# A new planned order of loads, squares and stores in a DMA-heavy attention and mixture-of-adapters kernel: 16 stores in place of 19

## The chip, the cores and the metric

The kernel runs on one core of a Trainium2 chip. The metric is the device time of one launch in microseconds (us); lower is better. The core's engines are called PE (TensorE, matmul), PEld (its weight loads), DVE (VectorE), ACT (ScalarE), POOL (GpSimd) and SP (SyncE); 16 DMA engines move data between device memory (HBM) and the on-chip memory.

## The reference

```python
B, N, C = (4, 6400, 256)                     # q, k, v: float32 [B, N, C]
def _attn_ref(q, k, v, tau):
    qn = q / (np.linalg.norm(q, axis=1, keepdims=True) + 1e-06)
    kn = k / (np.linalg.norm(k, axis=1, keepdims=True) + 1e-06)
    s = kn.transpose(0, 2, 1) @ qn / tau     # [B, C, C]: attention between channels
    s = s - s.max(-1, keepdims=True)
    a = np.exp(s)
    a /= a.sum(-1, keepdims=True) + 1e-09
    return (v @ a).astype(np.float32)

def _moe_ref(x, w_gate, A, B):               # x = attention output as [25600, 256]; 8 experts, rank 16
    logits = x @ w_gate
    topk = np.argpartition(-logits, K, axis=1)[:, :K]          # K = 2
    ...
    w = np.exp(sel)                          # sel: the two chosen logits less their maximum
    w /= w.sum(-1, keepdims=True) + 1e-09
    ...
            z = x[mask] @ A[e]
            delta[mask] += w[mask, k, None] * (z @ B[e])
    return (x + delta).astype(np.float32)
```

Per batch, a 256x256 matrix of products of k and q is summed over all 6400 rows, divided by the column norms of k and q, and turned into a softmax `a`. Then each row of v is multiplied by `a`, and a gated sum of two of eight rank-16 adapters is added.

## The kernel before

**Layout.** The 6400 rows of a batch lie on 128 partitions, 50 rows ("columns" below, 256 numbers each) per partition. q and k of a batch come in two halves of 25 columns (`QK`); v and the output are cut into 5 pieces of 10 columns (`PC` = 10, `NP` = 5). A piece is written (b, i): batch, number in the batch. One column is 128 KB in float32.

**Loads.** Every load of q, k and v but the first two goes out on POOL's queue (L690) and turns float32 into bf16 on the way; the profile counts its bytes on the bf16 side. `WORDS` is the order of the loads: q31 is the second half of q and k of batch 3, v12 the third load of v of batch 1. `V` says which pieces one load of v brings: (2, 2) is pieces 2 and 3 in one load of 20 columns. `PARTS` cuts a half of q and k into several loads. A load waits on POOL until its slot is free: there are 4 slots for halves of q and k, and 4 for pieces of v.

**Batch stage.** For each column, PE adds the product of k and q to an accumulator (step `G`, L705). The squares for the norms come in one of two ways, chosen per batch, group of five columns and q or k: as further matmuls of `G` (L709 for k, L713 for q), or, for the entries of `OFF`, as a Square on ACT (L726) and an addition on DVE (L732), summed up at the end and brought in by a small matmul (`n2p`, L747). After the last column a chain of small steps on PE, DVE and ACT makes the softmax `a` and `waA`, that is `a` times gate weights and adapters.

**Piece stage.** Per piece: transposes of v on PE (`T`, L890) and their copy out (L872 on ACT or L874 on DVE); gate logits and adapter inputs in one go, twenty matmuls (`ZL`, L914), for pieces in `MERGED`, otherwise logits first (`log`, L928) and the adapter inputs later (`Z`, L981); the gate on DVE and ACT; the gated inputs (L992); their transposes (`gzT`, L1004); then per two columns the output, v times `a` plus the adapters (`Y`, L1017 and L1022), and its copy into one of 7 output slots (`Ye`, L872 or L874).

**Stores.** A store (L1033) goes out on SP's queue. A piece in `PAIRS` is stored together with the next one, in one store of 20 columns from two neighbouring slots. `FINE` cuts pieces of the last batch into several stores. `HOLD` names a load, and the store is not issued until that load has landed:

```python
def held_by(p, b, i):
    kind, d, j = HOLD[b, i]
    return [k for k in p.steps if k[:4] == ("load", kind, d, load_of(d, j) if kind == "v" else j)][-1]
```

(0, 3): ('k', 3, 1) thus holds piece (0, 3) until the second half of k of batch 3 has landed; with kind 'v' the third number is a piece, and the load is the one that brings it.

**The order.** All of it is laid out when the program is built. `Plan.run` is a list scheduler with given costs: each engine takes, of the steps that are ready and find their slots free, the one with the lowest rank. A rank is a place in the order of loads: `G` has the place of its half, the steps of a piece that of its load, and the early steps of a piece (`T`, `ZL`, the gate) that place less `AHEAD`; squares have the place of their half less `SQ`. The engines then run the order so found, waiting on semaphores. Where PE has nothing to do the plan puts matmuls whose result nobody reads (`warm`, L880).

```python
p.add(("T", b, i, u), {"PE": 0.109 * n + 0.001}, [("load", "v", b, v, c0 * PC, n0 * PC)], x - ahead, ...)
p.add(("sq", w, b, g), {"ACT": 0.106 + 0.2133 * n}, ..., pos["qk", b, i] - SQ, ...)
...
parts = FINE[i] if b == B - 1 and i in FINE else ((0, PC * len(names)),)
for c, n in parts:
    p.add(("store", b, i, c, n), {"SP": 0.46}, ...)
```

Of the kernel before, what the change touches and what calls it, by code (L numbers as in the profile page):

```python
# [71 lines left out]
class Plan:  # L72
# [35 lines left out]
    def run(self, head):  # L108
# [137 lines left out]
UNITS = ((0, 4), (4, 4), (8, 2))  # L246
GATE = {"eq1": "ga", "t": "ga", "th": "ga", "g2": "ga", "lm": "gb", "mask": "gb"}
QK = ((0, 25), (25, 25))
V = (((0, 1), (1, 1), (2, 2), (4, 1)), ((0, 1), (1, 1), (2, 1), (3, 2)), ((0, 1), (1, 1), (2, 1), (3, 1),
        (4, 1)), ((0, 1), (1, 1), (2, 2), (4, 1)))  # L250
PAIRS = {(0, 1), (1, 0), (2, 0), (2, 3)}

GROUPS = ((0, 5), (5, 5), (10, 5), (15, 5), (20, 5), (25, 5), (30, 5), (35, 5), (40, 5), (45, 5))
ZUNITS = ((0, 3), (3, 3), (6, 2), (8, 2))
# [3 lines left out]
def group_of(c):  # L258
    return max(g for g, (c0, _) in enumerate(GROUPS) if c0 <= c)
# [6 lines left out]
def load_of(b, i):  # L266
    return max(g for g, (i0, _) in enumerate(V[b]) if i0 <= i)


def pieces(b, i):  # L270

    return next((((b, j), (b, j + 1)) for j in (i - 1, i) if (b, j) in PAIRS), ((b, i),))
# [8 lines that stand above are left out]
def make_plan(B, order, ahead):  # L281
# [6 lines left out]
    for kind, b, i in order:  # L288
        if kind == "v":
            c0, n = V[b][i]  # L290
            p.add(("load", "v", b, i, c0 * PC, n * PC), {}, (), 0, take=(("v", tuple((b, c0 + j) for j in range(n))),),
                  size=COL * n * PC)
            continue
        for c, n in PARTS.get((b, i), QK[i:i + 1]):
            for h in "qk":
# [3 lines left out]
    for h in "qk":  # L299
        p.add(("cast", h), {"ACT": 1.2}, [("load", h, 0, 0) + PARTS[0, 0][0]], 0)  # L300
    for b in range(B):

        for i, (c0, n) in enumerate(QK):
            for c in range(c0, c0 + n):
                deps = [k for k in p.steps if k[0] == "load" and k[2:4] == (b, i) and k[1] != "v"
                        and k[4] <= c < k[4] + k[5]]
                if (b, c) < (0, PARTS[0, 0][0][1]):
                    deps = [("cast", k[1]) for k in deps]
                if c:
                    deps.append(("G", b, c - 1))  # L310
                elif b:
                    deps += [(x, b - 1, ic) for x in ("n2", "accs") for ic in range(2)]
                p.add(("G", b, c), {"PE": 0.445 - 0.1135 * sum((b, group_of(c), w) in OFF for w in "kq")}, deps,
                      pos["qk", b, i] if b else -50,
# [3 lines left out]
        for w in "kq":  # L318
            halves = [x for x in range(len(GROUPS)) if (b, x, w) in OFF]
            if halves:  # L320
# [3 lines left out]
            for x, g in enumerate(halves):  # L324
# [3 lines left out]
                      [k for k in p.steps if k[:4] == ("load", w, b, i) and k[4] < c + n and c < k[4] + k[5]]  # L328
                      + [("cast", w)] * ((b, c) == (0, 0)), pos["qk", b, i] - SQ, take=(("ssq", ((w, b),)) if x == 0 else ("sq", ((w, b, g),)),),
                      give=(("qk", (w, b, i)),))  # L330
                if x:
                    p.add(("add", w, b, g), {"DVE": 0.069 + 0.2668 * n},
                          [("sq", w, b, g), before], pos["qk", b, i] - SQ, give=(("sq", (w, b, g)),))
                    before = ("add", w, b, g)
# [6 lines left out]
        if b == 0:  # L341
            p.add(("wts",), {"DVE": 2.12}, [("load", "k", 0, len(QK) - 1) + PARTS[0, len(QK) - 1][1]], -200)

# [21 lines left out]
        for i in range(NP):  # L365
            v = load_of(b, i)
            c0, n0 = V[b][v]
            x = pos["v", b, v] + 0.3 * (i - c0)
            for u, (c, n) in enumerate(UNITS):
# [4 lines left out]
                      [("T", b, i, u)], x - ahead, give=(("bank", ("T", b, i, u)),))  # L374
            merged = (b, i) in MERGED
            if merged:
# [54 lines left out]
    for b in range(B):  # L431
        for i in range(NP):
            x = pos["v", b, load_of(b, i)]
            names = pieces(b, i)
            if (b, i) != names[0]:
                continue
            parts = FINE[i] if b == B - 1 and i in FINE else ((0, PC * len(names)),)
            for c, n in parts:
                p.add(("store", b, i, c, n), {"SP": 0.46},
                      [("Ye", b, i + c0 // PC, c0 % PC) for c0 in range(c, c + n, 2)]  # L440
                      + ([held_by(p, b, i)] if (b, i) in HOLD else []), x, size=COL * n,
                      give=tuple(("y", x) for x in names) if c + n == PC * len(names) else ())
# [3 lines left out]
def make_order(words):  # L446

    order = [("qk", 0, i) for i in range(len(QK))]
    for w in words.split():
        order.append(("v" if w[0] == "v" else "qk", int(w[1]), int(w[2])))  # L450
    return order


WORDS = ('q10 v00 q11 v01 v02 q20 v03 v10 q21 v11 v12 v13 q30 v20 v21 v22 v23 q31 v24 v30 v31 v32 v33')
HEAD = 5.05
COL = 1.024 * 1.17647 / 32
WARM = 150
AHEAD = 5.7

HOLD = {(0, 0): ('v', 3, 2), (0, 1): ('v', 1, 4), (0, 2): ('v', 1, 2), (0, 3): ('k', 3, 1), (1, 0): ('v', 2,  # L460
        4), (1, 1): ('k', 3, 2), (1, 2): ('k', 3, 1), (1, 3): ('v', 3, 1), (2, 0): ('v', 3, 3), (2, 1):
        ('k', 2, 0), (2, 2): ('v', 1, 3), (2, 3): ('v', 2, 2), (3, 3): ('v', 2, 2)}

PARTS = {(0, 0): ((0, 5), (5, 12), (17, 8)), (0, 1): ((25, 17), (42, 8)), (3, 1): ((25, 17), (42, 8))}
FINE = {3: ((0, 6), (6, 4)), 4: ((0, 4), (4, 4), (8, 2))}
SPLIT, SHARES = set(), ()
OFF = {(0, 0, 'k'), (0, 0, 'q'), (0, 1, 'k'), (0, 2, 'k'), (0, 2, 'q'), (0, 3, 'k'), (0, 4, 'k'), (0, 4,
        'q'), (0, 5, 'q'), (0, 6, 'k'), (0, 7, 'k'), (0, 9, 'q'), (1, 0, 'k'), (1, 2, 'k'), (1, 3, 'k'), (1,
        3, 'q'), (1, 6, 'k'), (1, 6, 'q'), (1, 7, 'q'), (1, 8, 'k'), (1, 9, 'k'), (2, 0, 'k'), (2, 1, 'k'),
        (2, 3, 'k'), (2, 3, 'q'), (2, 4, 'k'), (2, 5, 'k'), (2, 5, 'q'), (2, 6, 'k'), (2, 6, 'q'), (2, 7,  # L470
        'q'), (2, 8, 'q'), (2, 9, 'q'), (3, 0, 'k'), (3, 1, 'k'), (3, 2, 'k'), (3, 2, 'q'), (3, 3, 'q'), (3,
        5, 'k'), (3, 5, 'q'), (3, 7, 'q'), (3, 8, 'q'), (3, 9, 'q')}
SQ = 0
SAFE = 1.3
MERGED = {(0, 0), (0, 1), (0, 2), (0, 3), (0, 4), (1, 0), (1, 1), (1, 2), (1, 3), (1, 4), (2, 0), (2, 2),
        (2, 3), (2, 4), (3, 0), (3, 1), (3, 2), (3, 3), (3, 4)}


def first_ahead(nc, names):
# [90 lines left out]
def kernel(  # L570
# [72 lines left out]
    scrap = const.tile([1, 16], BF16, name="scrap")  # L643
    order = make_order(WORDS)
    plan = make_plan(B, order, AHEAD)
    steps = plan.run(HEAD)
# [5 lines left out]
    def sb(s, kind, name, shape, dtype, part=""):  # L652

        if (kind, name, part) not in held:
            held[kind, name, part] = sbuf.tile(
                shape, dtype, tag=f"{kind}{at[kind, name]}{part}", name=f"{kind}{part}")
        return held[kind, name, part]
# [41 lines left out]
    def do_G(s, b, c):  # L699
# [4 lines left out]
        for ic in range(CC):  # L704
            nc.tensor.matmul(  # L705
                acc[ic][:, 0:256], kt[:, j, ic::CC], qt[:, j, :],
                start=c == 0, stop=False, skip_group_check=True)
            if (b, group_of(c), "k") not in OFF:
                nc.tensor.matmul(  # L709
                    acc[ic][:, 256:384], kt[:, j, ic::CC], kt[:, j, ic::CC],  # L710
                    start=False, stop=False, skip_group_check=True)
        for ic in range(0 if (b, group_of(c), "q") in OFF else CC):
            nc.tensor.matmul(  # L713
# [42 lines left out]
    def do_n2(s, b, ic):  # L756
# [5 lines left out]
        for x, w in enumerate("kq"):  # L762
            if all((b, g, w) in OFF for g in range(len(GROUPS))):
                continue
# [6 lines left out]
    def do_rsqrt(s, b):  # L771
        n2 = st[b]["n2"]
        for x, w in enumerate("kq"):
            part = held.get(("bank", ("n2p", w, b)))
            if part is None:
                continue
            if all((b, g, w) in OFF for g in range(len(GROUPS))):
                nc.vector.tensor_copy(n2[:, x, :], part)
# [97 lines left out]
    def do_cast(s, what):  # L876
        nc.scalar.copy(held["qk", (what, 0, 0), ""][:, 0:PARTS[0, 0][0][1], :], W[what])  # L877

# [23 lines left out]
    def gate_tiles(s, b, i):  # L902
        for part in ("log", "ga", "gb"):
            sb(s, "gate", (b, i), [P, PC, E], FP32, part)
        for part in ("m1", "m2", "msum"):
            sb(s, "gate", (b, i), [P, PC], FP32, part)
# [30 lines left out]
    def gate_step(name):  # L937
        def f(s, b, i):
            if (b, i) in MERGED and name == "m1":
                gate_tiles(s, b, i)  # L940
            g = {part: held["gate", (b, i), GATE.get(part, part)]
                 for part in ("log", "m1", "eq1", "lm", "m2", "msum", "t", "th", "mask", "g2")}
            if (b, i) in MERGED:
                g["log"] = held["zl", (b, i), ""][:, :, 0:E]
# [41 lines left out]
    def do_Ze(s, b, i, u):  # L986
        c, n = UNITS[u]
        gz = sb(s, "gz", (b, i, u), [P, n, ER], BF16)
        z = held["zl", (b, i), ""][:, c:c + n, E:] if (b, i) in MERGED else held["bank", ("Z", b, i, u)]
        pairs = gz.rearrange("p c d -> p (c d)").rearrange("p (h x two) -> p h two x", two=2, x=ER)  # L990
# [37 lines left out]
    def do_store(s, b, i, c, n):  # L1028
# [3 lines left out]
        for rows in SHARES if (b, i) in SPLIT else (P,):  # L1032
            r = nc.sync.dma_start(out_v[b, p:p + rows, lo:lo + n, :], Y[p:p + rows, at_y:at_y + n, :])  # L1033
            if (b, i) in HOLD and not p:
                tc.add_manual_dep(r.ins, loaded[held_by(plan, b, i)],
# [62 lines left out]
```

## Time and profile before

| | |
|---|---|
| time of the kernel, median of 3 runs | 251.12 us (251.01 to 251.16) |
| span of the profiled execution, first to last instruction | 246.2 us |
| around the span, to the median | 4.9 us (the last store is issued at 244.8 us and lands in 5.1 us) |
| busy PE, DVE, ACT | 218.3, 184.8, 169.7 us |
| DMA | 65.85 MB in 8788 packets as the queues count it; HBM read 78.91 MB, written 26.21 MB |
| loads on POOL's queue | 39: 17 of v, 11 of q, 11 of k |
| stores on SP's queue | 19: 4 of 20 columns, 10 of 10, 1 of 6, 3 of 4, 1 of 2 |
| mean granted TensorE clock | 0.965 |

The profile is of one execution. Its view by slices cuts the span into 40 parts and gives the busy share of each engine in tenths, then that of the DMA engines and what they moved; one DMA engine can hold packets of two queues at a time, so that a share can be over 1. The view by windows gives busy microseconds per engine in stretches of our choice, the granted clock, the DMA share and GB/s. The view of waits names who waited for whom. Each DMA queue has a line with its packets, megabytes and the share of the 16 engines' time that the packets took: q0 carries POOL's loads, q1 SP's stores, q8 instructions.

### The profile page before, as it was taken

The page shows a single profiled execution, that of the slowest core. Times are in us where ns is not written, and L with a number is a line of the kernel's source. Part 1 is how long each engine was busy: PE and PEld are TensorE (multiplying, and loading weights), DVE is VectorE, ACT ScalarE, POOL GpSimd, SP SyncE. Part 2 cuts the span into 40 slices and gives each one's busy share as a digit, 9 for nine tenths or more (in the row PEclk, how much of TensorE's full clock was granted, in tenths as well). Part 3 has the DMA queues.
Part 4 walks back from the last instruction along what each step waited for, and adds up shares of the span by engine and source line. Part 5 has one row for each costly group of instructions (what it writes and reads, how often), then busy time and mean ns, then how long its engine had stood idle before and what let it go on. Part 6 is the DMA issues. An engine that isn't in the chain of part 4 may idle for free.

```text
span 246.2 us, 5334 instructions
## 1 busy us (share of the span) xinstructions
PE 218.3 (89%) x2208; PEld 179.7 (73%) x2025; DVE 184.8 (75%) x511; ACT 169.7 (69%) x316; POOL 21.8 (9%) x45
## 2 busy tenths in 40 slices
PE   0687298498999999999969999999999999999996
PEld 0255175176877998978959788899776799999985
DVE  0045578558869689999974898998989578788681
ACT  2944442275666769888776787999453599988885
POOL 7000202100030011000201003110000000000000
PEclk9999769679999999999997999999999999999999
DMA  8999999999999999999999999999999999999999
GB/s 275 215 216 216 208 221 227 201 225 219 206 220 224 209 210 231 208 224 201 260 281 268 316 276 207 216 217 223 308 216 303 380 373 282 323 407 433 419 429 409
DMA packets 8788, 65.85 MB, mean 268 GB/s; under 512 B 994, under 2 KB 1378, under 8 KB 4796
## 3 DMA queue, kind: packets, MB, share of 16 engines
q0 software_dynamic: 5616, 38.67, 75.4%
q1 hardware_dynamic: 2812, 26.06, 25.6%
q10 hardware_dynamic: 336, 0.79, 0.8%
q8 instruction: 16, 0.26, 0.4%
q14 instruction: 8, 0.07, 0.1%
HBM read 78.91 MB, written 26.21 MB: 427 GB/s over the span
## 4 chain that ended last, share of the span: by engine, by line
DMA 39%; PE 37%; issue 11%; DVE 9%; ACT 3%; POOL 1%; POOLq 0%; ACTq 0%
DMA v<-in_v_dram 27%; PE Y_ps L1017 10%; DMA qk<-in_q_dram 6%; PE acc L705 6%; PE Y_ps L1022 5%; PE ZL_ps L914 5%; DMA qk<-in_k_dram 5%; PE T_ps L890 5%; PE gzT_ps L1004 3%; DVE gz L992 3%; DVE ssq L732 2%; PE acc L709 2%; ACT y L872 1%; DVE y L874 1%; PE acc L713 1%
## 5 line engine op out<-in xcount | busy, mean ns | idle before, releaser
L705 PE MATMUL acc<-qk 128*128 128x256 bf16 x400 | 77.6, 288 | 15.3 <-ACT qk L877 8.3
L732 DVE TENSOR_TENSOR ssq<-ssq,sq 128x1280 f32<-128x1280 f32 x35 | 52.0, 1487 | 21.9 <-ACT sq L726 21.9
L705 PEld LDWEIGHTS <-qk 128*128 128x128 bf16 x400 | 39.7, 104 | 31.0 <-DMA qk<-in_k_dram 9.8
L872 ACT COPY y<-Y_ps 128x512 f32<-128x512 f32 x87 | 50.8, 594 | 15.2 <-PE Y_ps L1022 12.9
L726 ACT ACTIVATE sq<-qk 128x1280 f32<-128x1280 bf16 x35 | 44.8, 1279 | 23.5 <-DVE ssq L732 20.7
L1017 PE MATMUL Y_ps<-a_bf,vT 128*128 128x256 bf16 x400 | 60.0, 272 | 0.1
L1017 PEld LDWEIGHTS <-vT 128*128 128x128 bf16 x400 | 38.3, 98 | 5.1 <-issue 0.4
L1022 PE MATMUL Y_ps<-ball,gzT 128*128 128x256 bf16 x200 | 38.2, 273 | 0.0
L992 DVE TENSOR_TENSOR gz<-zl,gatega 128x256 bf16<-128x256 f32 x95 | 35.4, 444 | 0.5
L709 PE MATMUL acc<-qk 128*128 128x128 bf16 x170 | 32.7, 225 | 0.0
L890 PE MATMUL T_ps<-ident,v 128*128 128x128 f32 x200 | 27.2, 284 | 3.9 <-DMA v<-in_v_dram 3.6
L713 PE MATMUL acc<-qk 128*128 128x128 bf16 x200 | 28.7, 227 | 0.0
L872 ACT COPY vT<-T_ps 128x512 f32<-128x512 f32 (+1 forms) x47 | 23.0, 545 | 5.5 <-PE T_ps L890 5.4
L890 PEld LDWEIGHTS T_ps<-ident,v 128*128 128x128 f32 x200 | 22.9, 146 | 5.3 <-issue 3.3
L914 PE MATMUL ZL_ps<-waA_sb,vT 128*128 128x136 bf16 x380 | 26.3, 223 | 0.4 <-ACT y L872 0.3
L914 PEld LDWEIGHTS <-vT 128*128 128x128 bf16 x380 | 23.8, 98 | 1.4 <-issue 0.4
L713 PEld LDWEIGHTS <-qk 128*128 128x128 bf16 x200 | 19.1, 102 | 5.0
L872 ACT COPY zl<-ZL_ps 128x408 f32<-128x408 f32 (+1 forms) x50 | 19.9, 457 | 3.4 <-PE ZL_ps L914 3.4
L1004 PE MATMUL gzT_ps<-ident,gz 128*128 128x128 f32 x100 | 19.8, 281 | 1.8 <-DVE gz L992 1.5
L1022 PEld LDWEIGHTS <-gzT 128*128 128x128 bf16 x200 | 19.5, 98 | 2.3
L874 DVE COPY zl<-ZL_ps 128x272 f32<-128x272 f32 (+1 forms) x26 | 12.7, 498 | 6.8 <-PE ZL_ps L914 6.6
L690 POOL DMA_DIRECT2D qk<-in_q_dram x11 | 6.1, 552 | 111.8 <-ACT y L872 41.2
(78 smaller groups left out, 217.2 us busy)
## 6 DMA issues: line engine op xcount, KB each, us to landing
out_dram<-y SPq DMA_DIRECT2D x10, 1280.0 KB, 11.8
out_dram<-y SPq DMA_DIRECT2D x4, 2560.0 KB, 17.5
v<-in_v_dram POOLq DMA_DIRECT2D x14, 640.0 KB, 28.0
qk<-in_q_dram POOLq DMA_DIRECT2D x5, 1600.0 KB, 15.9
qk<-in_k_dram POOLq DMA_DIRECT2D x5, 1600.0 KB, 23.0
v<-in_v_dram POOLq DMA_DIRECT2D x3, 1280.0 KB, 28.5
qk<-in_q_dram POOLq DMA_DIRECT2D x2, 1088.0 KB, 19.5
qk<-in_k_dram POOLq DMA_DIRECT2D x2, 1088.0 KB, 25.0
```

The costliest lines, as they stand in the source:

```text
L705: nc.tensor.matmul(acc[ic][:, 0:256], kt[:, j, ic::CC], qt[:, j, :], start=c == 0, stop=False, skip_group_check=True)
L709: nc.tensor.matmul(acc[ic][:, 256:384], kt[:, j, ic::CC], kt[:, j, ic::CC], start=False, stop=False, skip_group_check=True)
L713: nc.tensor.matmul(acc[ic][:, 384:512], qt[:, j, ic * P:(ic + 1) * P], qt[:, j, ic * P:(ic + 1) * P], start=False, stop=c == NC - 1, skip_ ...
L726: nc.scalar.activation(out[:, 0:n, :], t[:, j:j + n, :], ACT.Square)
L732: nc.vector.tensor_tensor(out=t, in0=t, in1=held["sq", (w, b, g), ""][:, 0:n, :], op=OP.add)
L872: nc.scalar.copy(out, in_)
L890: nc.tensor.matmul(ps[:, j, :], vt[:, c + j, :].bitcast(FP32), W["ident32"], is_transpose=True, start=(j == 0), stop=(j == n - 1))
L914: nc.tensor.matmul(ps[:, j, :], vT_of(b, i, c + j)[:, :, ic], st[b]["waA"][:, ic, :], start=(j == 0 and ic == 0), stop=(j == n - 1 and ic ...
L992: nc.vector.tensor_tensor(out=pairs[:, h].rearrange("p c (e r) -> p c e r", e=E), in0=z[:, 2 * h:2 * h + 2, :].rearrange("p c (e r) -> p c ...
L1004: nc.tensor.matmul(ps[:, j, :], pairs[:, j * P:(j + 1) * P], W["ident32"], is_transpose=True, start=(j == 0), stop=(j == n // 2 - 1))
L1017: nc.tensor.matmul(ps[:, j, :], vT_of(b, i, c + j)[:, :, ic], st[b]["a"][:, ic, :], start=(j == 0 and ic == 0), stop=False, skip_group_che ...
L1022: nc.tensor.matmul(ps[:, j, :], pair[:, :, j], W["B"], start=False, stop=(j == 1), skip_group_check=True)
```

## The change

Only the constants that feed the planner differ; no function is changed. Stores: five pairs in place of four, and of the last batch only piece (3, 4) is cut, in 6 and 4 columns, where (3, 3) was cut in 6 and 4 and (3, 4) in 4, 4 and 2. Loads: two loads of v are merged with a neighbour, and the first half of q and k of batch 1 comes in two parts each, so there are 39 as before; `v00` comes ahead of `q10`, and q31 one piece of v earlier. `HOLD` has 19 entries in place of 13, most with other loads. `OFF` has 40 entries in place of 43, differently spread over the batches (k and q together: 8, 8, 12, 12 in batches 0 to 3; before 12, 9, 12, 10). `MERGED` lacks three pieces in place of one. `AHEAD` and `SQ` change the ranks of early piece steps and squares.

```diff
--- before.py
+++ after.py
@@ -246,9 +246,9 @@
 UNITS = ((0, 4), (4, 4), (8, 2))
 GATE = {"eq1": "ga", "t": "ga", "th": "ga", "g2": "ga", "lm": "gb", "mask": "gb"}
 QK = ((0, 25), (25, 25))
-V = (((0, 1), (1, 1), (2, 2), (4, 1)), ((0, 1), (1, 1), (2, 1), (3, 2)), ((0, 1), (1, 1), (2, 1), (3, 1),
-        (4, 1)), ((0, 1), (1, 1), (2, 2), (4, 1)))
-PAIRS = {(0, 1), (1, 0), (2, 0), (2, 3)}
+V = (((0, 1), (1, 1), (2, 2), (4, 1)), ((0, 1), (1, 2), (3, 2)), ((0, 1), (1, 2), (3, 1), (4, 1)), ((0,
+        1), (1, 1), (2, 2), (4, 1)))
+PAIRS = {(0, 1), (1, 0), (1, 2), (2, 0), (2, 2)}
 
 GROUPS = ((0, 5), (5, 5), (10, 5), (15, 5), (20, 5), (25, 5), (30, 5), (35, 5), (40, 5), (45, 5))
 ZUNITS = ((0, 3), (3, 3), (6, 2), (8, 2))
@@ -451,29 +451,32 @@
     return order
 
 
-WORDS = ('q10 v00 q11 v01 v02 q20 v03 v10 q21 v11 v12 v13 q30 v20 v21 v22 v23 q31 v24 v30 v31 v32 v33')
+WORDS = ('v00 q10 q11 v01 v02 q20 v10 v03 q21 v11 v12 v20 q30 v21 q31 v22 v23 v30 v31 v32 v33')
 HEAD = 5.05
 COL = 1.024 * 1.17647 / 32
 WARM = 150
-AHEAD = 5.7
-
-HOLD = {(0, 0): ('v', 3, 2), (0, 1): ('v', 1, 4), (0, 2): ('v', 1, 2), (0, 3): ('k', 3, 1), (1, 0): ('v', 2,
-        4), (1, 1): ('k', 3, 2), (1, 2): ('k', 3, 1), (1, 3): ('v', 3, 1), (2, 0): ('v', 3, 3), (2, 1):
-        ('k', 2, 0), (2, 2): ('v', 1, 3), (2, 3): ('v', 2, 2), (3, 3): ('v', 2, 2)}
-
-PARTS = {(0, 0): ((0, 5), (5, 12), (17, 8)), (0, 1): ((25, 17), (42, 8)), (3, 1): ((25, 17), (42, 8))}
-FINE = {3: ((0, 6), (6, 4)), 4: ((0, 4), (4, 4), (8, 2))}
+AHEAD = 10.6
+
+HOLD = {(0, 0): ('v', 3, 2), (0, 1): ('v', 1, 1), (0, 2): ('v', 3, 0), (0, 3): ('k', 3, 1), (0, 4):
+        ('k', 3, 0), (1, 0): ('k', 3, 1), (1, 1): ('v', 1, 2), (1, 2): ('v', 3, 1), (1, 3): ('v', 2, 0),
+        (1, 4): ('k', 3, 0), (2, 0): ('v', 2, 0), (2, 1): ('k', 3, 0), (2, 2): ('v', 2, 2), (2, 3):
+        ('v', 2, 2), (2, 4): ('k', 2, 0), (3, 0): ('v', 3, 1), (3, 1): ('k', 3, 1), (3, 2): ('v', 3, 0),
+        (3, 4): ('v', 3, 0)}
+
+PARTS = {(0, 0): ((0, 5), (5, 10), (15, 10)), (0, 1): ((25, 17), (42, 8)), (1, 0): ((0, 17), (17, 8)),
+        (3, 1): ((25, 17), (42, 8))}
+FINE = {4: ((0, 6), (6, 4))}
 SPLIT, SHARES = set(), ()
-OFF = {(0, 0, 'k'), (0, 0, 'q'), (0, 1, 'k'), (0, 2, 'k'), (0, 2, 'q'), (0, 3, 'k'), (0, 4, 'k'), (0, 4,
-        'q'), (0, 5, 'q'), (0, 6, 'k'), (0, 7, 'k'), (0, 9, 'q'), (1, 0, 'k'), (1, 2, 'k'), (1, 3, 'k'), (1,
-        3, 'q'), (1, 6, 'k'), (1, 6, 'q'), (1, 7, 'q'), (1, 8, 'k'), (1, 9, 'k'), (2, 0, 'k'), (2, 1, 'k'),
-        (2, 3, 'k'), (2, 3, 'q'), (2, 4, 'k'), (2, 5, 'k'), (2, 5, 'q'), (2, 6, 'k'), (2, 6, 'q'), (2, 7,
-        'q'), (2, 8, 'q'), (2, 9, 'q'), (3, 0, 'k'), (3, 1, 'k'), (3, 2, 'k'), (3, 2, 'q'), (3, 3, 'q'), (3,
-        5, 'k'), (3, 5, 'q'), (3, 7, 'q'), (3, 8, 'q'), (3, 9, 'q')}
-SQ = 0
+OFF = {(0, 2, 'q'), (0, 3, 'q'), (0, 5, 'q'), (0, 6, 'k'), (0, 7, 'k'), (0, 7, 'q'), (0, 8, 'q'), (0, 9,
+        'q'), (1, 0, 'q'), (1, 1, 'k'), (1, 1, 'q'), (1, 2, 'k'), (1, 2, 'q'), (1, 5, 'q'), (1, 7, 'k'),
+        (1, 8, 'q'), (2, 0, 'k'), (2, 0, 'q'), (2, 2, 'k'), (2, 2, 'q'), (2, 3, 'k'), (2, 3, 'q'), (2,
+        4, 'k'), (2, 5, 'q'), (2, 6, 'k'), (2, 7, 'k'), (2, 7, 'q'), (2, 9, 'q'), (3, 0, 'k'), (3, 1,
+        'k'), (3, 1, 'q'), (3, 3, 'k'), (3, 3, 'q'), (3, 4, 'k'), (3, 4, 'q'), (3, 5, 'k'), (3, 6, 'k'),
+        (3, 7, 'q'), (3, 8, 'k'), (3, 8, 'q')}
+SQ = -5.75
 SAFE = 1.3
-MERGED = {(0, 0), (0, 1), (0, 2), (0, 3), (0, 4), (1, 0), (1, 1), (1, 2), (1, 3), (1, 4), (2, 0), (2, 2),
-        (2, 3), (2, 4), (3, 0), (3, 1), (3, 2), (3, 3), (3, 4)}
+MERGED = {(0, 0), (0, 1), (0, 2), (0, 3), (0, 4), (1, 0), (1, 1), (1, 2), (1, 4), (2, 0), (2, 1), (2,
+        2), (2, 4), (3, 0), (3, 1), (3, 2), (3, 3)}
 
 
 def first_ahead(nc, names):
```

## The prediction

> **What bounds the kernel now.** I read the page's slices first.
>
> ```profile
> PE   0687298498999999999969999999999999999996
> ...
> DMA  8999999999999999999999999999999999999999
> ...
> HBM read 78.91 MB, written 26.21 MB: 427 GB/s over the span
> ```
>
> The DMA row is at nine tenths or more in every slice but the first. The bytes read and written, 105.1 MB, over the span of 246.2 us make the 427 GB/s. The order changes no byte, so a DMA system without idle time is a floor under any order. PE is nearly as full. The view by windows (busy us and instructions of PE, granted clock, DMA share, GB/s) says where it is not:
>
> ```profile
> 44.00:50.00 6.00, 2.80 (x8) 0.58 0.96 201
> ...
> 60.00:120.00 60.00, 57.48 (x614) 1.00 1.03 216
> 120.00:130.00 10.00, 7.67 (x80) 1.00 1.04 282
> 130.00:193.50 63.50, 62.51 (x687) 0.97 1.03 259
> ...
> 198.50:244.30 45.80, 45.36 (x473) 1.00 1.01 382
> ```
>
> From 60 us on PE idles for 6 us in all, and in the last 45.8 us for 0.4. The DMA share never falls under 0.96 after the first 10 us. The waits of PE after 50 us are short:
>
> ```profile
> PE T_ps L890 <- DMA v<-in_v_dram: 3.6, 4, 2.3
> PE gzT_ps L1004 <- DVE gz L992: 1.5, 3, 0.9
> PE ZL_ps L914 <- ACT y L872: 0.3, 1, 0.3
> ```
>
> Two resources are full at once; the end decides which one counts. The DMA view of 247 to 250 us, 40 cells of 0.075 us:
>
> ```profile
> DMA  8868659293949493666747565544422220000000
> ...
> q1 hardware_dynamic: 225, 0.60, 49.7%
> ```
>
> Until 247 us all 16 engines are busy; then one after another runs dry, the last at about 249.5 us. The last store was issued at 244.8. Sixteen engines with equal rows thus end 2.5 us apart, and the slowest sets the time. It had a queue, so it was not waiting for PE.
>
> **The change, part by part.** The sum is made against the profiled execution: span 246.2 us, slowest DMA engine dry at 249.5, and 1.6 us more to the median of 251.1, which I take as this execution's time (the three runs lie within 0.15 us).
>
> *Three stores fewer.* Two windows hold stores alone, of 20-column rows (20,480 bytes) from 228 to 231 us, of 10-column rows (10,240 bytes) from 235 to 237:
>
> ```profile
> DMA packets 65, 1.29 MB, mean 430 GB/s; under 512 B 2, under 2 KB 2, under 8 KB 2
> ...
> q1 hardware_dynamic: 65, 1.29, 100.4%
> ```
>
> ```profile
> DMA packets 90, 0.84 MB, mean 420 GB/s; under 512 B 8, under 2 KB 8, under 8 KB 8
> ...
> q1 hardware_dynamic: 90, 0.84, 99.4%
> ```
>
> First window: 1.004 x 16 x 3 us = 48.2 us of packet time for 63 rows (the two small packets are semaphore writes): 765 ns a row. Second: 0.994 x 16 x 2 = 31.8 us for 82 rows: 388 ns. Two short rows cost 11 ns more than one long one. A store has 128 rows, 8 on each engine: 0.09 us per store saved, with its semaphore write 0.1. From below: the packet records in the trace overlap by some 4 ns, and from one landing to the next a 20-column store takes 6.06 us, a 10-column store 3.05, so that 0.04 us is saved. Three stores: 0.1 to 0.3 us, all on the path, since DMA is never idle. I take 0.2, the middle of two readings. SP's issue (0.33 us each) hides: SP waits up to 114 us for a store's data.
>
> The Trainium skill's DMA: Bandwidth & Descriptors, section Anatomy of one DMA, gives each DMA on POOL's path a fixed 2.0 us beside its bytes. If stores cost that and paid it one after another, three fewer would save 6 us, and the sum would be 245. The rows above say that under a full queue the fixed part is hidden behind other packets.
>
> *Loads.* Two merges of v (two 10s into a 20) and two cuts (25 columns into 17 and 8, for q and k): the number of rows is the same, so I book nothing; the 22 ns that a row costs beside its bytes (398 ns for 5,120 bytes against 774 for 10,240) are paid as often as before.
>
> *The end.* The last store has 4 columns in place of 2; (3, 3) leaves whole, at 240.0 (its second part goes then) and no longer from 238.8. Four columns are 0.52 MB, at 420 GB/s 1.25 us of every engine. For the slowest engine to end at 249.5, this store must begin on it by 248.3; the 6 columns ahead (1.9 us) by 246.4; the 10 of (3, 3) (3.05 us) by 243.3. The first transfer of the run was issued at 0.0 and moved its first packets after 1.0 us. With unchanged compute the issues are at 244.8, 243.5 (two output steps of 0.66 us earlier) and 240.0: slack 2.5, 1.9 and 2.3 us. Booked at zero: the queue is the cover, and past it each us costs a us.
>
> The skill's Perfetto Trace Analysis, section DMA Optimizations, says that splitting lets parts start sooner if the DMA engines are generally idle; by that rule a last store twice as long would cost 0.6 us more. Here they aren't idle before 247.
>
> *PE.* On PE a group of squares costs 0.11 us per column (0.44 us against 0.33 from column to column of `G`), 0.56 a group; on ACT 1.28 and on DVE 1.49. `OFF` brings PE 4 groups in batch 0 (+2.2 us), 1 in batch 1 (+0.6), none in batch 2, and takes 2 in batch 3 (-1.1). Two pieces more outside `MERGED`: `log` 0.48 plus `Z` 1.11 in place of `ZL` 1.18, +0.4 each. Sum +2.5 us. Batch 0's 2.2 hide: from 14 to 50 us PE is busy for 25.5 of 36. The other 0.3 land in full stages. Against it stands `v00` ahead of `q10`: before, PE's first matmul of batch 1 is at 50.9, behind loads that landed at 48 to 50; with the first 17 columns of q10 and k10 in loads of their own, and v00 before them, there is work 2 us earlier. PE's end moves by between -2 and +2.5 us. I take 0: most of the surplus lies where PE waited for loads. ACT loses 3 x 1.28 and DVE 3 x 1.49 us of squares, and two pieces' copies of `ZL` (1.8 us each) shrink to one of 0.23; both have over 45 us to spare, so nothing is booked.
>
> *Holds.* The held stores are fed when a load lands, as before; before k31 lands, 4 pieces are free to go in the old order ((0, 4), (0, 1) with (0, 2), (1, 4)), and the same 4 in the new one. POOL's queue is in order, too: a load whose slot is late keeps all loads behind it. Before, the longest such wait was 30 us without the DMA share falling. Booked at 0; it can cost up to the 2.3 us that PE once waited for v.
>
> Sum: 251.1 - 0.2 = 250.9.
>
> **Rivals.**
>
> *A: DMA stays full, as above: 250.9*, 250.7 to 251.4 with the bounds of the stores and half a us of stalls.
>
> *B, slower: compute ends too late.* PE and DMA are both full, and a new order can cost PE 2.5 us (all moved work uncovered) to 4.8 (a 2.3 us stall, as at 120 to 130, on top). It decides from 1.9 us on, the smallest slack above: 0.6 to 2.9 us late, less 0.2: 251.5 to 253.8, middle 252.6. For it: 0.4 us idle on PE in the last 45.8, and coarser stores at the end. Against: the 10 us of waiting early in the run.
>
> *C, slower: one more instruction packet on the slowest engine.*
>
> ```profile
> q8 instruction: 16, 0.26, 0.4%
> ```
>
> Equal rows can't make engines end 2.5 us apart; these 16 packets of 16 KB can. Each takes 0.9 to 1.0 us of one engine (0.4% of 16 x 246 us, over 16), and in the packet records the one at 32.8 us leaves a single engine 0.9 us behind the rest for good. Two or three on one engine are the 2.5 us. PE has 2208 + 2025 instructions, 265 per packet; the change adds some 90 (3 groups, the pieces outside `MERGED`), a third of a packet. One more on the slowest engine: 251.8.
>
> *D, faster: the packets fall better.* They go out when PE reaches them, and the order shifts that. One fewer on the slowest engine: 250.9 - 0.9 = 250.0. Spread evenly, one on each, all engines would end 0.9 us after the 247 of those that had none, at 247.9 and not at 249.5: no order gets below 250.9 - 1.6 = 249.3.
>
> *E: the change does not do what it says.* Twenty pieces less five pairs make 15 stores, plus one for the cut piece: 16. The diff settles it.
>
> **How the numbers follow.** A 0.34, B 0.26, C 0.12, D 0.28. Two tenths of a per cent, about what a measurement of this kernel can tell from no change, are 0.5 us, so A is "same" (250.6 to 251.6), D faster, B and C slower. The likeliest is A, 250.9. The range goes from 249.9, below D, to 252.7, at the middle of B.
>
> **What would show it.** Right: a DMA share at or above 0.96 in every window to 246 us, the packet rows above at the same 765 and 388 ns, and engines that run dry one after another behind the last issue. B shows as full cells right up to the last store's own packets, all engines ending together, and an issue of the last store after 246.7. C or D shows as another width of the fall after the last full cell, at the same issue time. I am wrong in the main if the DMA share drops in mid-run: then holds or late loads starve the queues, and the missing share is the loss.

## The result, and the profile after

The changed kernel takes 252.12 us (median of 20 runs, 251.95 to 252.44). The kernel before, run beside it, has a median of 251.35 us, and its runs fall into two groups: 12 of 20 at 251.0 to 251.5, 8 at 251.8 to 252.3. The ratio is 1.0023, 95% interval 1.0014 to 1.0032 (the two medians alone would give 1.0031): slower by 0.23%, just past the 0.2% that I had set as a bound. Beside the first three runs of before it is 1.0 us. I had forecast 250.9 and a tiny gain. The time lies in the stated range, but on the other side.

The page of the changed kernel, slices and instruction queue:

```profile
span 245.8 us, 5380 instructions
...
PE   0698188498989999989979999999989999999996
...
DMA  8999999999999999999999999999999999999999
...
q8 instruction: 17, 0.28, 0.4%
HBM read 78.91 MB, written 26.21 MB: 428 GB/s over the span
```

The instructions end 0.4 us sooner than before (245.8 for 246.2), and DMA is as full. The one line that reads worse is q8: 17 packets of instructions, where there were 16. The same windows as for the kernel before (busy us and instructions of PE, granted clock, DMA share, GB/s):

```profile
44.00:50.00 6.00, 3.39 (x18) 0.79 1.02 209
60.00:120.00 60.00, 57.18 (x613) 1.00 1.02 216
120.00:130.00 10.00, 8.43 (x84) 1.00 1.02 306
130.00:193.50 63.50, 62.15 (x687) 1.00 1.03 264
...
198.50:244.30 45.80, 45.30 (x490) 1.00 1.01 381
```

PE works as tightly as before: 0.5 us idle in the last stage, for 0.4. The longest wait of PE after 50 us is shorter (1.5 us for 2.3), but the waits come to as much as before, 5.5 us in all for 5.4:

```profile
PE T_ps L893 <- DMA v<-in_v_dram: 2.1, 2, 1.5
PE gzT_ps L1007 <- DVE gz L995: 1.5, 3, 0.7
PE acc L708 <- DMA qk<-in_k_dram: 0.8, 1, 0.8
PE ZL_ps L917 <- ACT zl L875: 0.6, 1, 0.6
PE Y_ps L1020 <- ACT waA_sb L861: 0.3, 1, 0.3
PE ZL_ps L917 <- DVE waA_sb L863: 0.2, 1, 0.2
```

Long rows go as fast as before. From 224.9 to 228 us (20-column rows), then from 235 to 237 (10-column rows):

```profile
DMA packets 68, 1.37 MB, mean 443 GB/s; under 512 B 1, under 2 KB 1, under 8 KB 1
...
q1 hardware_dynamic: 68, 1.37, 103.4%
```

```profile
DMA packets 91, 0.84 MB, mean 420 GB/s; under 512 B 9, under 2 KB 9, under 8 KB 9
...
q1 hardware_dynamic: 91, 0.84, 99.3%
```

1.034 x 16 x 3.1 us over 67 rows is 765 ns, 0.993 x 16 x 2 us over 82 rows 388 ns: the numbers of before. What differs is the last us. The DMA view of 226 to 252 us in cells of 0.65 us; in the kernel before the row ends in "328 293 258 151 9 0 0 0":

```profile
GB/s 410 473 410 425 441 425 293 441 394 410 454 425 394 441 457 410 410 473 425 378 457 425 394 435 441 425 394 394 432 403 407 400 356 284 249 104 32 13 0 0
...
q8 instruction: 2, 0.03, 0.5%
```

The fall from 400 GB/s starts at the same place, but there is a tail of "32 13": about one engine of 16 at work (427 / 16 = 27 GB/s) after the others are done. In the packet records the other engines finish the last store by 249.6 us, as before, and one at 250.4. The second of the two q8 packets in this view went out at 241.0 us, 0.96 us long: 16 KB of instructions, in the middle of the last stores. Both last stores land later than without it, as the first experiment shows. Issues by size, with the median us from issue to landing:

```profile
out_dram<-y SPq DMA_DIRECT2D x1, 768.0 KB, 6.4
out_dram<-y SPq DMA_DIRECT2D x1, 512.0 KB, 6.3
```

So the theory to test: **the 17th packet of PE instructions falls on a DMA engine that ends late anyway, and costs 0.9 us**. Rivals: **the coarser stores at the end** cost it, or **the rest of the order** (`v00` first, the holds, the new pairs).

### The profile page after: what moved, and what is told of

It reads as the page before. It is cut to its first block, busy times and chain, and to the rows that moved or that the text cites. A ratio compares the mean times of both kernels' runs of the same rounds, so it can differ in the third digit from the quotient of the medians.

```text
span 245.8 us, 5380 instructions
## 1 busy us (share of the span) xinstructions
PE 217.4 (88%) x2273; PEld 176.4 (72%) x2046; DVE 183.0 (74%) x514; ACT 162.4 (66%) x301; POOL 21.5 (9%) x45
## 4 chain that ended last, share of the span: by engine, by line
PE 48%; DMA 39%; DVE 6%; ACT 4%; issue 1%; POOL 1%; POOLq 0%
DMA v<-in_v_dram 36%; PE Y_ps L1020 12%; PE T_ps L893 7%; PE acc L708 6%; PE Y_ps L1025 6%; PE ZL_ps L917 5%; PE gzT_ps L1007 4%; DMA qk<-in_q_dram 3%; DVE ssq L735 3%; PE acc L712 2%; ACT sq L729 1%; PE Z_ps L984 1%; PE acc L716 1%; PE n2p_ps L750 1%; ACT zl L875 1%
## 5 line engine op out<-in xcount | busy, mean ns | idle before, releaser
L708 PE MATMUL acc<-qk 128*128 128x256 bf16 x400 | 80.3, 286 | 18.3 <-DMA qk<-in_k_dram 9.7
L735 DVE TENSOR_TENSOR ssq<-ssq,sq 128x1280 f32<-128x1280 f32 x32 | 47.5, 1486 | 28.2 <-ACT sq L729 28.0
L708 PEld LDWEIGHTS <-qk 128*128 128x128 bf16 x400 | 40.4, 105 | 35.6 <-DMA qk<-in_k_dram 12.2
L875 ACT COPY y<-Y_ps 128x512 f32<-128x512 f32 x83 | 48.0, 592 | 15.1 <-PE Y_ps L1025 12.7
L729 ACT ACTIVATE sq<-qk 128x1280 f32<-128x1280 bf16 x32 | 41.0, 1280 | 25.1 <-DMA qk<-in_q_dram 12.5
L712 PE MATMUL acc<-qk 128*128 128x128 bf16 x220 | 45.0, 232 | 0.0
L995 DVE TENSOR_TENSOR gz<-zl,gatega 128x256 bf16<-128x256 f32 x85 | 31.3, 444 | 0.4
L716 PE MATMUL acc<-qk 128*128 128x128 bf16 x180 | 25.5, 224 | 0.0
L917 PE MATMUL ZL_ps<-waA_sb,vT 128*128 128x136 bf16 x340 | 23.7, 223 | 0.8 <-ACT zl L875 0.6
L716 PEld LDWEIGHTS <-qk 128*128 128x128 bf16 x180 | 15.9, 100 | 5.3 <-issue 0.9
L875 ACT COPY zl<-ZL_ps 128x408 f32<-128x408 f32 (+1 forms) x40 | 16.5, 461 | 4.3 <-PE ZL_ps L917 4.1
L875 ACT COPY gzT<-gzT_ps 128x256 f32<-128x256 f32 (+1 forms) x36 | 12.1, 339 | 7.3 <-PE gzT_ps L1007 6.8
```

The costliest lines, as they stand in the source:

```text
L708: nc.tensor.matmul(acc[ic][:, 0:256], kt[:, j, ic::CC], qt[:, j, :], start=c == 0, stop=False, skip_group_check=True)
L712: nc.tensor.matmul(acc[ic][:, 256:384], kt[:, j, ic::CC], kt[:, j, ic::CC], start=False, stop=False, skip_group_check=True)
L716: nc.tensor.matmul(acc[ic][:, 384:512], qt[:, j, ic * P:(ic + 1) * P], qt[:, j, ic * P:(ic + 1) * P], start=False, stop=c == NC - 1, skip_ ...
L729: nc.scalar.activation(out[:, 0:n, :], t[:, j:j + n, :], ACT.Square)
L735: nc.vector.tensor_tensor(out=t, in0=t, in1=held["sq", (w, b, g), ""][:, 0:n, :], op=OP.add)
L875: nc.scalar.copy(out, in_)
```

## The experiments

**Fewer PE instructions in the changed kernel.** Matmuls for squares are left out in three groups of q and four of k, all of batch 0.

```diff
+LESS = {"q": {(0, 0), (0, 1), (0, 4)}, "k": {(0, 0), (0, 1), (0, 2), (0, 3)}}
...
-            if (b, group_of(c), "k") not in OFF:
+            if (b, group_of(c), "k") not in OFF and (b, group_of(c)) not in LESS["k"]:
...
```

> Leaves out the matmuls for the squares of q of three groups and of k of four groups in batch 0, 103 PE instructions in all; the rest of the changed kernel stands. Packet theory (the 17th packet of PE instructions, late, on a nearly slowest DMA engine, costs the time): 16 packets on q8, last DMA packet at about 249.6 us, time 251.1 to 251.3. End-store rival (the coarser stores at the end cost it): 17 or 16 packets, time stays at 252.1. Order rival (v00 first, the holds, the new pairs cost it): stays at 252.1.

Measured: 251.15 us (12 runs, 250.92 to 251.30); ratio to the kernel before 0.998 (0.9968 to 0.9992). Its page and its last two stores:

```profile
q8 instruction: 16, 0.26, 0.4%
```

```profile
out_dram<-y SPq DMA_DIRECT2D x1, 768.0 KB, 5.4
out_dram<-y SPq DMA_DIRECT2D x1, 512.0 KB, 5.3
```

The stores land 1.0 us sooner after their issue than in the changed kernel. Same order, pairs, holds and end stores, 1.0 us less: both rivals miss. But 3 us of PE work went too, so the reverse was needed.

**More PE instructions in the kernel before.** The same PE work in more pieces, for 27 of the 30 unread matmuls:

```diff
+CUT = 27
...
-        nc.tensor.matmul(bank(s, ("warm", n), [P, 512], FP32), W["ident"], W["ident"][:, None, :].to_broadcast([P, 4, P]),
-                         start=True, stop=True)
+        ps = bank(s, ("warm", n), [P, 512], FP32)
...
+        for j in range(4):
+            nc.tensor.matmul(ps[:, j * P:(j + 1) * P], W["ident"], W["ident"], start=(j == 0), stop=(j == 3),
+                             skip_group_check=True)
```

> The kernel before with 27 of its 30 unread matmuls cut into four of a quarter of the width, 81 (88 with weight loads) more PE instructions and the same PE work. Packet theory: 17 packets on q8 and 0 to 0.9 us more than before, 252.0 if the 17th falls on an engine that ends late, as in the changed kernel. End-store and order rivals: as before, 251.1 to 251.3.

Measured: 252.01 us (251.74 to 252.30), with

```profile
q8 instruction: 17, 0.28, 0.4%
```

The old order with one packet more has the time of the new one, and no run under 251.7. (Its ratio to the kernel before, 1.0012, 0.9996 to 1.0028, is blurred by that kernel's two groups.)

**The end stores, both ways.** In one kernel the old order takes the new cut, `FINE = {4: ((0, 6), (6, 4))}`; in the other the new order takes the old one.

> The kernel before with the changed kernel's cut of the last pieces alone ((3, 3) whole, (3, 4) in 6 and 4): 17 stores, PE instructions as before. Packet theory: 16 packets, 251.0 to 251.3. End-store rival: 251.9 to 252.2. Order rival: as before.

> The changed kernel with the old cut of the last pieces ((3, 3) in 6 and 4, (3, 4) in 4, 4 and 2): 18 stores. Packet theory: 17 packets, 252.0 to 252.3. End-store rival: 251.1 to 251.4. Order rival: 252.1.

Measured: 251.67 us (250.97 to 252.29) for the old order with the new cut, ratio 1.000 (0.9983 to 1.0017), six of twelve runs at 251.0 to 251.3 and six at 252.0 to 252.3: two groups, like the kernel before; the upper six miss what the packet theory expected of it. And 252.10 us (251.76 to 252.41) for the new order with the old cut, where the changed kernel has 252.12. The coarser stores cost nothing that shows. Nor does their saving: two stores more or fewer move nothing beyond the interval.

**Where the limit lies.** The kernel before had two groups of times, and its packet count might sit on the edge. Counting PE instructions in the program: before 3875, changed 3961, the first experiment 3858. Seven unread matmuls cut into four (+21), or the last ten left out (-20):

> The kernel before with 7 of its unread matmuls cut into four, 21 more PE instructions (3896 in the program; before 3875, changed 3961, the first experiment 3858). If the limit at which a 17th packet is fetched lies at about 3918, where the changed kernel's trace puts it: 16 packets, 251.1 to 251.5, spread as before. If the kernel before already sits on the limit, which would explain why its own times fall at 251.1 and at 252.2: 17 packets, 252.0 in all runs. End-store and order rivals: as before.

> The kernel before without the last ten of its unread matmuls, 20 PE instructions fewer (3855). Packet theory with the kernel before on the limit: 16 packets and 251.0 to 251.3 in every run, no run near 252.2. If its two times have another cause: as scattered as before.

Measured: 252.33 us (251.86 to 252.60) with 21 more, 251.20 us (251.00 to 251.44) with 20 fewer, 12 runs each, and neither has the other's group. Their lines for q8, with 21 more and with 20 fewer:

```profile
q8 instruction: 17, 0.28, 0.4%
```

```profile
q8 instruction: 16, 0.26, 0.4%
```

Twenty-one instructions that add no work are worth a microsecond here, and the limit lies between 3858 and 3896, nearer than the 3918 that I had read from the changed kernel's trace.

**The kernel before, run again.** Single runs with a profile, to find one of the upper group:

> The kernel before, unchanged, for one more profile. Packet theory: if the time is near 251.2, 16 packets; if near 252.2, a 17th packet in the last few us, and one DMA engine that ends some 0.9 us after the others.

> The kernel before, unchanged. Packet theory: if its time is near 252.2, the profile has a 17th packet on q8 in the last few us; if near 251.2, 16 packets. If 252.2 comes with 16 packets, its two times have another cause.

Four more had the same expectation. Four of the six took 251.13, 251.29, 251.62 and 251.67 us, and none has a packet on q8 after 233.2 us; why two of these lie 0.3 to 0.5 us above the other two, without a packet more, is open. The two others took 252.72 and 252.48. DMA view of the first of these, 246 to 252 us:

```profile
GB/s 437 423 410 437 382 369 341 410 273 246 273 246 259 218 218 246 260 232 232 259 191 109 55 27 27 27 27 27 14 27 27 27 14 0 0 0 0 0 0 0
...
q8 instruction: 1, 0.02, 1.0%
```

A 17th packet, at 247.1 us (248.0 in the other), and then one engine alone at 27 GB/s until 250.96. PE's last matmul is over by then for 3.8 us (it ends at 243.3). So it seems that the end of PE's instruction stream asks for the packet; no view names what does. In a run of the lower group (251.13 us) the same view reads:

```profile
GB/s 437 410 396 396 396 369 341 287 300 287 287 300 300 287 219 246 246 232 205 178 109 82 27 0 0 0 0 0 0 0 0 0 0 0 0 0 0 0 0 0
```

Why the old program fetches it in some runs and not in others isn't shown.

**When the packet is fetched.** In the changed kernel all 25 unread matmuls are cut into four, so that each packet comes some 75 instructions sooner.

> The changed kernel with its 25 unread matmuls cut into four: 75 more PE instructions (4048, the next limit is near 4131), each packet fetched some 75 instructions sooner. Packet theory: still 17 packets; 251.9 to 252.4 if a 17th packet anywhere late in the run falls on an engine that ends late, 251.2 to 251.6 if it is fetched early enough to find one with slack.

Measured: 252.04 us (251.68 to 252.46), 17 packets, the last at 238.4 us for 241.0. Coming 2.6 us sooner does not help.

**Fifteen packets.** Like the first experiment, but with 10 groups of q and 16 of k left out.

> Leaves out the matmuls for the squares of q of 10 groups and of k of 16 groups in batches 0 to 2, 370 PE instructions (3591) and some 14 us of PE. Packet theory: 15 packets, 250.2 to 251.1, depending on whether one packet less falls on the slowest engine. PE as the second bound: much more than that, 249 or less, since PE ends up to 14 us earlier. Order rival: stays at 252.1.

Measured: 251.05 us (250.90 to 252.08), 15 packets; PE was busy for 208.7 us, 8.7 less than in the changed kernel (I had put 14), and its span was no shorter (246.5 us). Ten of the twelve runs lie at 250.9 to 251.3, 0.1 us from the 251.15 of the first experiment with its 16 packets. So not every packet counts: taking away the 16th did not make the last engine end sooner. The other two took 251.99 and 252.08 us; they have no profile, and why they lie there is open. The test says little on PE as a second bound, since PE's end did not move.

**The old `MERGED` in the new order, planned anew.** It was meant as another way to fewer PE instructions.

```diff
-MERGED = {(0, 0), (0, 1), (0, 2), (0, 3), (0, 4), (1, 0), (1, 1), (1, 2), (1, 4), (2, 0), (2, 1), (2,
-        2), (2, 4), (3, 0), (3, 1), (3, 2), (3, 3)}
+MERGED = {(0, 0), (0, 1), (0, 2), (0, 3), (0, 4), (1, 0), (1, 1), (1, 2), (1, 3), (1, 4), (2, 0), (2, 2),
+        (2, 3), (2, 4), (3, 0), (3, 1), (3, 2), (3, 3), (3, 4)}
```

> The changed kernel with the old MERGED, so that two pieces more take ZL in place of log and Z; 3892 PE instructions, planned anew. Packet theory with the limit near 3918: 16 packets, 251.1 to 251.4; with the limit near 3875: 17, 252.0. Order rival (pairs, holds, v00): 252.1.

Measured: 257.60 us (257.22 to 258.09), ratio 1.0237 (1.0211 to 1.0263), a miss for all three theories. Its windows, with the columns as above:

```profile
190.00:200.00 10.00, 9.95 (x87) 0.83 1.02 313
...
240.00:246.00 6.00, 5.96 (x57) 1.00 0.62 261
```

This is my rival B: compute ends 7 us late (the last store is issued at 251.6 us), and the DMA share drops to 0.62. In the new order neither of the two shows. A stretch of 10 us at a granted clock of 0.83 can explain some 1.7 us of the delay, by my estimate; what else in the plan caused it, I did not follow. It has 17 packets, too.

**The new order with 16 packets and nothing left out.** Seven more groups of squares go off PE, piece (3, 4) into `MERGED`, and the planner runs again:

```diff
-AHEAD = 10.6
+AHEAD = 9.77
...
+OFF |= {(0, 0, 'k'), (0, 0, 'q'), (0, 1, 'k'), (0, 1, 'q'), (0, 8, 'k'), (2, 6, 'q'), (3, 5, 'q')}
...
+MERGED.add((3, 4))
```

> The changed order planned once more with seven more groups of squares off PE, piece (3, 4) in MERGED and AHEAD 9.77, nothing left out: 16 stores, 3823 PE instructions. Packet theory: 16 packets on q8, 250.9 to 251.3 in every run. Order rival (pairs, holds, v00): 252.1.

Measured: 250.94 us (250.89 to 251.30), ratio to the kernel before 0.9973 (0.9959 to 0.9987). It has 16 packets on q8. In the DMA view of 226 to 252 us it ends without a tail, and its last stores land 1.4 us sooner after their issue than in the changed kernel:

```profile
GB/s 359 473 347 441 425 378 394 410 457 410 425 457 378 441 441 410 451 362 331 425 473 394 394 425 441 394 425 473 366 406 410 410 429 262 239 63 0 0 0 0
```

```profile
out_dram<-y SPq DMA_DIRECT2D x1, 768.0 KB, 5.0
out_dram<-y SPq DMA_DIRECT2D x1, 512.0 KB, 4.9
```

It beats both kernels: 1.2 us (0.5%) under the changed one, and under the kernel before by 0.1% to 0.4%. Most of the latter is that kernel's upper group; against its lower group alone (12 of the 23 runs beside it, median 251.24) it is 0.3 us. It is a new plan, so that its gain over the changed kernel need not be the packet's alone; the pair with 21 more and 20 fewer has no such doubt.

## Why the prediction was wrong

**The floor was right.** DMA is full to the end in the changed kernel, as A said; PE's end (last matmul over at 243.8 us, before 244.2) and the rows stood where the sum had them. With 16 packets the new order takes 250.94 us planned anew and 251.15 with matmuls left out, and the sum said 250.9; that the first agrees to 0.05 us is luck, as no part of the 0.2 us in the sum was seen by itself.

**The cost of the stores was small, as said, and can't be seen.** Exchanging the end cuts moved nothing beyond the interval, against the 0.1 us a store that the rows gave as a ceiling. At the fixed 2.0 us that the Trainium skill's DMA: Bandwidth & Descriptors, section Anatomy of one DMA, gives for a DMA on POOL's path, two stores paid one after another would have been an estimated 4 us.

**The step that failed is C: "265 per packet; the change adds some 90 (...), a third of a packet".** The mechanism, its price (0.9 us) and the count (2273 + 2046 instructions after, 86 more) held. But the sum has no term for it: it books nothing where the runs show 0.9 to 1.0 us, and that turned a small gain into a loss. I turned a third of a packet into a small chance, as if the place of the limit were unknown. It could be read to within some 50 instructions. In the trace of before the last packet goes out at 232.8 us, and the view by windows counts what PE did after it (PE, then its weight loads):

```profile
232.80:246.20 13.40, 11.06 (x104) 9.30 (x102) 7.20 (x23) 9.67 (x20) 0.00 (x0) 1.00 1.00 418
```

That is 206 instructions. From 32.8 to 232.8 us, 15 packets had come for 3827 of them (4233 less 200 before and 206 after), one for each 255. With 86 more, 292 stand behind the last packet, over 255: a 17th was all but certain. (255 is not the limit itself: with 206 behind it the kernel before fetches a 17th in some runs, and with 21 more in all.) The chance that I left to it, 0.12, should have been most of the forecast, at 251.8; measured are 252.1. That a late packet would meet an engine that ends late could not be read there.

The Trainium skill's Runtime: NRT & Kernel Launch, section Instruction fetch mechanics, says that each engine fetches its instructions in 16 KiB blocks of 256 and that crossing a block is mostly hidden. The block agrees with this case (17 packets in 0.28 MB, one per 255 instructions); that it is hidden does not, where DMA is full to the end: 0.9 to 1.0 us.

**The two groups of the kernel before** I had not seen: its three runs lay within 0.15 us. It stood within 21 instructions of the limit, and in the upper group it takes as long as the changed kernel. Measured against its lower group the change costs 0.9 us, against its upper group nothing.

**D and the spread of the engines.** I put the 2.5 us between the first engine that runs dry and the last wholly down to the packets. With 15 packets the last engine still ends at 249.6 us. What else sets them apart stays open. The packet records hold one hint: the lengths of the q8 packets recur nearly alike after every eight in all traces (in the changed kernel 0.97, 0.98, 0.96, 0.89, 0.89, 0.95, 0.95, 0.94 us, then 0.97, 0.96, 0.96, 0.88, 0.88, 0.94, 0.93, 0.93, and the 17th 0.96). If packets go round the engines in turn, 16 may give each engine one, a 17th gives one engine a second, and 16 packets would not set the engines apart at all. No record names a packet's engine, so this is not shown.

## What to carry to other kernels

Where DMA is busy to the last microsecond, everything that crosses the DMA engines counts, instructions too: count the packets of the instruction queue, and how many instructions stand behind the last one, before giving an engine more of them. Near the mean distance between two packets the count is a warning and not yet an answer: here the limit came some 50 instructions sooner. When a change moves the time by a fixed step whatever its size, look for a count that crosses a limit, and test it by adding and taking away instructions that do no work. A kernel whose own runs fall into two groups may sit on such a limit.

## What the runs showed that I had not expected

Forty-one PE instructions without any use, 21 added in one kernel and 20 taken away in the other, are 1.1 us apart (252.33 against 251.20 us). A packet of PE instructions can still go out 3.8 us after PE's last matmul (at 247.1 us), and the launch waits for the engine that carries it. And a small edit of the planner's constants, with 69 PE instructions fewer, cost 5.5 us, far more than any term of my sum.
